# A new issue order for every engine of a fused sparse-attention and MoE kernel, annealed with added latency on transfers

## The chip, the cores and the metric

The kernel runs on one core of a Trainium2 chip. The metric is the device time of one execution in microseconds (us). The engines are TensorE (PE in the profile, its weight loads PEld), VectorE (DVE), ScalarE (ACT), GpSimd (POOL) and SyncE (SP), which here only issues transfers. Each engine works through its own queue strictly in the order in which the program gives it instructions. An instruction whose inputs are not there holds up everything behind it on the same engine.

## The reference, cut to what matters

```python
# q, k, v: (4, 8, 768, 64) f32;  w_in: (512, 2048), w_out: (2048, 512) f32
k_min, k_max = min and max of k over chunks of 32 keys            # 24 chunks
ub   = sum_d max(q*k_min, q*k_max);  ub = where(causal chunk, ub, -1e9)
sel  = the 6 chunks of largest ub for each query
scores = where(sel and causal, q @ k.T / 8, -1e9)
attn = softmax(scores) @ v
x    = attn.transpose(0, 2, 1, 3).reshape(3072, 512)
h    = x @ w_in
out  = (h * clip(h + 3, 0, 6) / 6) @ w_out
```

## The kernel before, in words

The 32 heads are worked in 16 pairs, numbered 0 to 15, four pairs to a batch. The 3072 tokens of the MoE part are worked in 8 groups of 384, two groups to a batch, so a group can start when its batch's four pairs are done. Attention of later batches and MoE of earlier ones are interleaved.

The whole kernel is a list of 1158 tokens, `ORDER`, and a loop that calls one small function for each token, in that order. Nothing reorders afterwards: each function issues its instructions on one engine, so `ORDER`, read for the tokens of one engine, is that engine's queue. Two tokens of different engines may stand in any order as long as a producer stands ahead of its reader.

The tokens, with the engine that runs them (`i` is a pair, `g` a group, a last letter is the PSUM slot: `a`, `b`, `c` are two banks each, `x`, `y` one bank each):

- SP: `lk.i`, `lq.i`, `lv.i` load K, Q, V (two, two and one transfers); `wl.n` loads a quarter of a weight matrix (0 to 3 of w_in, 4 to 7 of w_out); `sm.i` writes a selection mask to DRAM (four transfers) and `ml.i.j` reads it back spread over the rows of key block j; `xt.g` transposes a group's attention output (three transfers); `st.g.t` writes 128 rows of the result (256 KB).
- PE: `K.i`, `Q.i` transpose K and Q; `U.i` (or `ud.i` for two pairs at once) the chunk bounds; `T.i` transposes them, `L.i` the selection; `S.i.u` scores of unit u (six units to a pair); `A.i`, `B.i.e` the products with V for the first and second half of the queries; `X.g.n` transposes for groups 0 and 1; `H.g.f` eight matmuls of the first MoE product; `O.g.t.n` four matmuls of the second one, four such tokens making one output tile of 128 rows. `Z` is a warm-up.
- ACT: `kb`, `qb` copy K and Q out of PSUM as bf16; `rp` is relu(q); `ra` is relu(-q); `ex.i.u` the exponentials of a unit; `hu.g.f` the relu of the gate; `ot.g.t` copies an output tile from PSUM to the buffer that `st.g.t` sends.
- DVE: `mx`, `mn` chunk maxima and minima; `rn` is relu(-q) on this engine, instead of `ra`; `ub`, `us` add the causal bias; `t8` and `sel` select the chunks; `mt` the mask (for pairs 0 to 5 PE adds it to the scores); `mu.i.u` multiplies the exponentials by the mask (pairs 6 to 15); `na`, `nb` normalise; `gt.g.f` the gate's product.
- POOL: `vc.i` casts V, `wc.n` casts a weight quarter, `af.i.u` zeroes what lies above the diagonal in the exponentials, `am.i.j` in the mask.

The buffers that tie the queues together: three PSUM slots of two banks for K, Q, U, S and H; two of one bank for T, L, A, B, X and O; two V staging buffers and two weight staging buffers `WS` (which also hold masks later); and a ring of three output buffers `OT`. `ot` takes the next buffer of that ring, so the fourth `ot` in the list needs the store of the first to have landed:

```python
slot["OT", g, t] = OT[n_ot[0] % 3]
n_ot[0] += 1
```

Of the kernel before, what the change touches and what calls it, by code (L numbers as in the profile page):

```python
# [34 lines left out]
PRD Z.b.14 PRA PRP PRL lk.0 K.0.a kb.0 lq.0 Q.0.b lk.1 rp.0 qb.0 ra.0 K.1.c kb.1 mx.0 mn.0 U.0.a lq.1 Q.1.b rp.1  # L35
qb.1 ra.1 mx.1 ub.0 mn.1 T.0.x lq.2 Q.2.a rp.2 qb.2 U.1.c t8.0 sel.0 lk.2 K.2.b kb.2 lv.1 ub.1 L.0.y mt.0 rn.2
lv.0 S.0.0.c ex.0.0 T.1.x S.0.1.a mx.2 mn.2 ex.0.1 S.0.5.c ex.0.5 lk.4 lq.5 S.0.3.a ex.0.3 lq.4 t8.1 sel.1
S.0.2.b ex.0.2 af.0.1 lk.3 lq.3 U.2.c vc.0 lv.2 ub.2 af.0.5 S.0.4.a ex.0.4 L.1.y mt.1 S.1.5.c ex.1.5 T.2.x wl.1
S.1.1.b t8.2 sel.2 S.1.0.a ex.1.1 ex.1.0 af.0.0 vc.1 af.1.5 S.1.2.c ex.1.2 af.1.1 af.1.0 af.1.2 S.1.3.b ex.1.3
af.1.3 A.0.y L.2.x S.1.4.a ex.1.4 K.4.c mt.2 S.2.1.b Q.4.a kb.4 ex.2.1 na.0 A.1.x Q.3.b B.1.0.y B.1.1.y rp.4  # L40
qb.4 mx.4 mn.4 rp.3 qb.3 ra.3 K.3.c kb.3 rn.4 U.4.a vc.2 lv.3 lv.4 lk.5 lk.6 S.2.5.b ex.2.5 na.1 nb.1 ub.4 mx.3
wl.0 mn.3 af.0.2 S.2.0.a ex.2.0 T.4.x S.2.3.b ex.2.3 t8.4 S.2.4.a ex.2.4 sel.4 S.2.2.c ex.2.2 U.3.b ub.3 Q.5.a
rp.5 qb.5 L.4.y mt.4 lq.8 lk.7 T.3.x t8.3 S.4.0.b lq.6 lq.7 S.4.5.c ex.4.5 af.2.5 af.2.2 sel.3 rn.5 af.0.3
B.0.0.y wc.1 B.0.1.y nb.0 K.5.c L.3.x af.2.1 mt.3 S.4.1.a af.2.0 ex.4.0 kb.5 af.4.0 af.2.3 mx.5 mn.5 ex.4.1
af.4.1 S.4.3.b ex.4.3 X.0.0.y xe.0.0 S.4.2.a ex.4.2 af.4.3 vc.4 A.2.x na.2 wc.0 S.3.0.b ex.3.0 S.3.2.c ex.3.2
U.5.a S.3.3.b A.4.y ub.5 T.5.x na.4 ex.3.3 S.3.1.a ex.3.1 S.4.4.c ex.4.4 S.3.4.b vc.3 S.3.5.a af.3.1 ex.3.5
ex.3.4 t8.5 sel.5 B.2.0.y B.2.1.y L.5.x mt.5 af.4.2 af.4.5 af.3.0 af.3.2 af.3.5 af.3.3 bd K.7.c kb.7 S.5.2.a
nb.2 ex.5.2 A.3.x S.5.0.b ex.5.0 mx.7 mn.7 na.3 B.4.0.y K.6.a kb.6 S.5.5.b ex.5.5 lk.8 wl.2 lv.6 Q.6.c mx.6 mn.6
rp.6 qb.6 B.4.1.y nb.4 rn.6 Q.7.b rp.7 B.3.0.x S.5.1.a ex.5.1 B.3.1.x X.1.0.y qb.7 S.6.0.a ex.6.0 vc.6 wc.2
af.5.2 xe.1.0 wl.3 wc.3 lv.5 wl.4 lq.9 S.5.3.c ex.5.3 rn.7 X.0.1.y xe.0.1 S.7.0.b ex.7.0 nb.3 ud.6.a us.6 wl.5  # L50
lk.9 S.7.2.c ex.7.2 X.1.1.y vc.5 xe.1.1 S.7.1.b S.6.1.a ex.7.1 ex.6.1 af.5.1 af.7.1 af.5.0 af.5.3 af.5.5 wc.4
wc.5 T.6.x T.7.y t8.7 sel.7 t8.6 sel.6 S.6.2.c ex.6.2 S.6.4.b wl.6 ex.6.4 H.0.2.a hu.0.2 gt.0.2 S.5.4.c ex.5.4
H.0.5.b L.6.y L.7.x wc.6 af.7.0 S.6.3.c K.8.a mt.7 hu.0.5 gt.0.5 mt.6 ex.6.3 B.5.0.x kb.8 S.6.5.c mx.8 mn.8
ex.6.5 H.0.7.b hu.0.7 gt.0.7 Q.9.c sm.6 A.5.y na.5 rp.9 qb.9 rn.9 wl.7 H.0.6.a hu.0.6 gt.0.6 ml.6.3 ml.6.0
ml.6.2 H.1.2.b hu.1.2 gt.1.2 Q.8.c rp.8 qb.8 lk.10 rn.8 H.1.0.a hu.1.0 gt.1.0 K.9.b B.5.1.x kb.9 mx.9 mn.9
H.0.0.c hu.0.0 gt.0.0 H.0.1.a hu.0.1 gt.0.1 ud.8.b us.8 H.0.3.c S.8.1.a S.8.0.b ex.8.0 ex.8.1 hu.0.3 wc.7 am.6.3
af.8.0 nb.5 T.8.y O.0.2.0.x H.0.4.b hu.0.4 H.1.4.a t8.8 sel.8 L.8.y gt.0.3 mt.8 gt.0.4 O.0.2.1.x T.9.y t8.9
am.6.2 af.6.1 mu.6.5 sel.9 af.6.0 mu.6.0 hu.1.4 gt.1.4 ml.6.5 ml.6.1 sm.7 ml.6.4 am.6.5 mu.6.2 am.6.4 lq.10
ml.7.5 ml.7.3 ml.7.2 ml.7.4 am.7.4 lk.11 ml.7.0 am.7.2 am.7.5 S.7.4.c ex.7.4 S.8.2.b ex.8.2 mu.6.4 mu.6.1
O.0.2.2.x O.0.2.3.x ot.0.2 S.8.3.c S.8.4.b ex.8.3 ex.8.4 am.7.3 O.0.0.0.y O.0.0.1.y S.7.5.a S.7.3.c ex.7.5  # L60
S.8.5.b ex.8.5 ex.7.3 L.9.x O.0.0.2.y O.0.0.3.y ot.0.0 mu.6.3 mt.9 K.10.a kb.10 mx.10 ml.7.1 mn.10 Q.10.b A.6.x
B.6.0.y H.1.1.c rp.10 qb.10 ra.10 B.6.1.y na.6 hu.1.1 gt.1.1 S.9.1.a ex.9.1 S.9.5.b ex.9.5 O.0.1.0.x S.9.4.a
S.9.0.c S.9.3.b ex.9.3 ex.9.0 ex.9.4 O.0.1.1.x mu.7.5 O.0.1.2.x nb.6 mu.7.4 sm.8 K.11.b mu.7.1 kb.11 mu.7.0
mu.7.2 mu.7.3 O.0.1.3.x ot.0.1 lq.11 Q.11.c rp.11 qb.11 H.1.7.a lv.7 vc.7 af.8.1 mx.11 mn.11 A.7.y na.7 hu.1.7
gt.1.7 ra.11 ml.8.2 ml.8.4 ml.8.3 lq.12 af.9.1 am.8.4 af.9.0 sm.9 xt.2 ml.8.5 am.8.5 lk.12 B.7.0.x B.7.1.x
ml.8.1 ud.10.b nb.7 us.10 S.10.3.c ml.9.3 ml.8.0 ml.9.1 O.1.1.0.y S.10.1.a ml.9.2 ml.9.4 lv.8 st.0.2 ml.9.5
ex.10.3 ex.10.1 S.9.2.b S.10.2.c ex.10.2 ex.9.2 T.10.x t8.10 sel.10 H.1.3.a H.1.5.c hu.1.3 gt.1.3 T.11.x t8.11
sel.11 H.1.6.b hu.1.5 hu.1.6 gt.1.5 gt.1.6 O.1.1.1.y H.2.2.a H.2.7.c L.10.x K.12.b hu.2.2 gt.2.2 mt.10 Q.12.a
af.10.1 hu.2.7 am.8.2 am.8.3 kb.12 rp.12 L.11.x O.1.1.2.y O.1.1.3.y mu.8.5 mt.11 sm.10 gt.2.7 qb.12 mu.8.3 rn.12
mx.12 vc.8 ot.1.1 H.2.1.c mn.12 mu.8.0 mu.8.1 H.2.4.a mu.8.2 O.1.0.0.x O.1.0.1.x O.1.2.0.y H.2.5.b hu.2.4 gt.2.4  # L70
# [12 lines left out]
sel.12 S.13.1.a S.13.2.b ex.13.2 ex.13.1 O.2.1.3.x ot.2.1 B.11.0.y mn.14 B.11.1.y S.14.1.b ex.14.1 S.14.3.c
ex.14.3 nb.11 S.14.2.a ex.14.2 T.13.x lk.15 xt.3 lq.15 xt.5 t8.13 sel.13 L.12.y H.4.1.b hu.4.1 gt.4.1 H.4.0.c
hu.4.0 H.4.7.a hu.4.7 H.4.2.b hu.4.2 gt.4.0 gt.4.7 mt.12 gt.4.2 H.4.4.c hu.4.4 L.13.x H.3.3.a hu.3.3 H.4.3.b
hu.4.3 gt.4.4 gt.3.3 mt.13 lv.12 vc.12 sm.13 lv.13 gt.4.3 H.4.5.c Q.15.a O.4.1.0.y lv.14 sm.12 ml.13.2 st.2.2
st.2.1 ml.12.4 ml.13.0 hu.4.5 gt.4.5 rp.15 qb.15 rn.15 H.4.6.b hu.4.6 ml.12.1 ml.13.4 O.4.1.1.y gt.4.6 K.15.c
H.3.5.a kb.15 mx.15 mn.15 H.3.1.b ml.13.1 O.4.1.2.y O.4.1.3.y ml.13.3 hu.3.5 gt.3.5 hu.3.1 S.13.0.c ex.13.0
gt.3.1 vc.13 ot.4.1 st.4.1 af.13.1 am.12.4 S.14.4.a ud.14.b H.3.2.c am.13.4 vc.14 us.14 T.15.x t8.15 ex.14.4
sel.15 O.4.2.0.y H.3.6.b ml.13.5 ml.12.5 af.12.1 am.12.5 hu.3.6 gt.3.6 L.15.x H.3.0.a hu.3.0 O.4.2.1.y mt.15  # L90
hu.3.2 gt.3.0 T.14.x H.3.7.b H.3.4.a t8.14 sel.14 mu.13.3 ml.12.0 L.14.x O.4.2.2.y O.4.2.3.y hu.3.7 hu.3.4
gt.3.2 mt.14 O.4.0.0.x O.4.0.1.x O.4.0.2.x gt.3.4 O.4.0.3.x gt.3.7 ot.4.2 S.15.3.c S.14.5.a am.13.5 S.14.0.b
af.14.1 am.13.2 mu.12.1 ml.12.2 am.12.2 af.13.0 mu.13.0 ml.12.3 lv.15 am.12.3 mu.12.5 mu.12.4 mu.13.4 mu.12.0
mu.13.2 mu.12.2 mu.12.3 ex.14.0 ot.4.0 ex.14.5 am.13.3 mu.13.5 sm.14 sm.15 st.4.2 ml.14.3 ml.14.2 O.3.2.0.y
# [534 lines left out]
```

## Time and profile before

| | |
|---|---|
| five runs | 284.33, 284.71, 285.49, 287.11, 287.19 us; median 285.49 |
| the profiled execution | 283.86 us, of which the span of instructions is 282.1 |
| granted TensorE clock | 1.000 |
| busy: PE, DVE, ACT, POOL | 270.5, 195.5, 181.9, 73.8 us |
| moved by transfers | 54.38 MB |
| median time from issue to landing: K, Q, V | 4.6, 4.8, 5.8 us |
| the same: a weight quarter, a result store | 7.2 to 7.7, 3.4 us |

The profiled execution is the fastest of the six shown. The 1.8 us between its time and its span lie outside the first and last instruction. Times in the profile count from the start of the span.

### The profile page before, as it was taken

To read this page: it belongs to the slowest core of one execution; us is meant where nothing else is said; L and a number is where in the kernel's file an instruction comes from. 1 tells how busy PE (TensorE), PEld (TensorE's weight loads), DVE (VectorE), ACT (ScalarE), POOL (GpSimd) and SP (SyncE) were. 2 spreads that over 40 slices of the span, in tenths; PEclk is the share of its full clock that TensorE was granted. 3 is DMA by queue.
4 is the path that set the end of the run, shared out by engine and by line. 5 is a ranking of instruction groups with operands and counts; after the bars stand their busy time and mean duration, and the time that the engine had idled before them with its cause. 6 is when DMAs were issued, how large, how long until landed. Compare 5 with 4: busy or idle time off the path is not lost.

```text
span 282.1 us, 6868 instructions
## 1 busy us (share of the span) xinstructions
PE 270.5 (96%) x2670; PEld 162.4 (58%) x2692; DVE 195.5 (69%) x523; ACT 181.9 (64%) x241; POOL 73.8 (26%) x138
## 2 busy tenths in 40 slices
PE   8799999999999999989999999999999999999994
PEld 3567677756654665644655666555455646645541
DVE  4786997988889697879668877659636774625310
ACT  2899999998758897625978876553357522424421
POOL 6043289195451230223142001106315000000000
PEclk9999999999999999999999999999999999999999
DMA  9999998989899998998999496899694120130102
GB/s 167 218 210 212 260 297 185 312 261 326 311 243 254 247 226 127 270 276 235 238 288 257 94 156 136 193 330 258 172 289 172 38 58 0 40 130 37 39 37 112
DMA packets 106911, 54.38 MB, mean 193 GB/s; under 512 B 86912, under 2 KB 95872, under 8 KB 106880
## 3 DMA queue, kind: packets, MB, share of 16 engines
q1 hardware_dynamic: 106880, 53.95, 78.1%
q8 instruction: 21, 0.34, 0.5%
q14 instruction: 10, 0.08, 0.1%
HBM read 42.34 MB, written 9.24 MB: 183 GB/s over the span
## 4 chain that ended last, share of the span: by engine, by line
PE 79%; ACT 8%; DVE 5%; DMA 5%; issue 3%; ACTq 0%
PE PSx L568 13%; PE PSy L568 12%; PE PBa L551 9%; PE PBb L551 9%; PE PBc L551 8%; DMA out_dram<-OT 5%; ACT PT L484 4%; PE PSy L507 3%; PE PSx L507 3%; PE PBa L470 2%; PE PBc L297 2%; PE PBa L297 2%; PE PBc L470 2%; PE PBb L470 2%; PE PBb L289 2%
## 5 line engine op out<-in xcount | busy, mean ns | idle before, releaser
L551 PEld LDWEIGHTS <-WIN 128*128 128x128 bf16 x512 | 48.9, 98 | 34.2 <-issue 1.7
L568 PEld LDWEIGHTS <-GT 128*128 128x128 bf16 x384 | 36.0, 98 | 41.5 <-issue 4.5
L568 PE MATMUL PSy<-WOUT,GT 128*128 128x512 bf16 x181 | 45.6, 379 | 2.2 <-ACT OT L576 1.4
L568 PE MATMUL PSx<-WOUT,GT 128*128 128x512 bf16 x181 | 45.2, 379 | 0.6 <-issue 0.2
L484 ACT ACTIVATE PT<-PBb 128x1024 bf16<-128x1024 f32 (+2 forms) x33 | 30.4, 921 | 7.8 <-PE PBb L470 7.5
L484 ACT ACTIVATE PT<-PBc 128x1024 bf16<-128x1024 f32 (+2 forms) x31 | 30.3, 978 | 7.4 <-PE PBc L470 4.6
L551 PE MATMUL PBa<-XT,WIN 128*128 128x384 bf16 x184 | 33.7, 326 | 0.1
L491 POOL TENSOR_SCALAR_AFFINE_SELECT PT<-PT 128x256 bf16<-128x256 bf16 x56 | 24.0, 449 | 33.4 <-ACT PT L484 29.7
L551 PE MATMUL PBb<-XT,WIN 128*128 128x384 bf16 x168 | 30.7, 326 | 0.0
L562 DVE SCALAR_TENSOR_TENSOR GT<-U,PBa 128x768 bf16<-128x768 bf16 x23 | 21.8, 949 | 12.7 <-ACT U L559 12.6
L551 PE MATMUL PBc<-XT,WIN 128*128 128x384 bf16 x160 | 29.3, 326 | 0.0
L462 DVE TENSOR_TENSOR PT<-PT,WS 128x768 bf16<-128x768 bf16 (+2 forms) x70 | 27.8, 442 | 1.9 <-POOL WS L455 1.9
L559 ACT ACTIVATE U<-PBc 128x768 bf16<-128x768 f32 x20 | 16.3, 813 | 19.8 <-PE PBc L551 19.7
L562 DVE SCALAR_TENSOR_TENSOR GT<-U,PBc 128x768 bf16<-128x768 bf16 x20 | 19.0, 951 | 13.2 <-ACT U L559 13.2
L484 ACT ACTIVATE PT<-PBa 128x1024 bf16<-128x1024 f32 (+2 forms) x32 | 27.7, 867 | 0.4 <-PE PBa L470 0.2
L292 POOL CAST VB<-VS 128x768 bf16<-128x768 f32 x16 | 13.3, 829 | 54.0 <-DMA VS<-in_v_dram 45.3
L559 ACT ACTIVATE U<-PBb 128x768 bf16<-128x768 f32 x21 | 17.0, 812 | 15.8 <-PE PBb L551 14.8
L507 PEld LDWEIGHTS <-PT 128*128 128x128 bf16 x672 | 24.1, 97 | 4.7 <-issue 1.8
L559 ACT ACTIVATE U<-PBa 128x768 bf16<-128x768 f32 x23 | 18.7, 811 | 11.7 <-PE PBa L551 10.2
L562 DVE SCALAR_TENSOR_TENSOR GT<-U,PBb 128x768 bf16<-128x768 bf16 x21 | 20.0, 951 | 6.0 <-ACT U L559 5.7
L470 PEld LDWEIGHTS <-KB 64*128 64x128 bf16 x320 | 14.2, 94 | 14.5 <-issue 10.3
L455 POOL TENSOR_SCALAR_AFFINE_SELECT WS<-WS 128x256 bf16<-128x256 bf16 x30 | 12.7, 437 | 30.3 <-DMA WS<-SCR 29.8
(118 smaller groups left out, 387.9 us busy)
## 6 DMA issues: line engine op xcount, KB each, us to landing
KSM<-in_k_dram SPq DMA_DIRECT2D x32, 192.0 KB, 4.6
QS<-in_q_dram SPq DMA_DIRECT2D x32, 192.0 KB, 4.8
VS<-in_v_dram SPq DMA_DIRECT2D x16, 384.0 KB, 5.8
out_dram<-OT SPq DMA_DIRECT2D x24, 256.0 KB, 3.4
WS<-in_moe_w_in_dram SPq DMA_DIRECT2D x4, 1024.0 KB, 7.2
WS<-in_moe_w_out_dram SPq DMA_DIRECT2D x4, 1024.0 KB, 7.7
SCR<-MTM SPq DMA_DIRECT2D x40, 72.0 KB, 3.6
MX<-SCR SPq DMA_DIRECT2D x10, 288.0 KB, 5.3
```

What stands on the lines that cost most here:

```text
L292: nc.gpsimd.tensor_copy(VB[i % 4][:, :, :, 0:D], VS[i % 2][:].rearrange("p e j d -> p j e d"))
L297: nc.tensor.transpose(flat[:, j * P:(j + 1) * P], src[:, j].rearrange("p e d -> p (e d)"), IDENT32[:])
L455: nc.gpsimd.affine_select(out=T, in_=T, pattern=[[0, 2], [1, P]], compare_op=A.is_ge, fill=0.0, base=0, channel_multiplier=-1)
L462: nc.vector.tensor_tensor(out=T, in0=T, in1=mask_view(i, j, lo, q0 + n), op=A.mult)
L470: nc.tensor.matmul(PSB[c][:, e, at:at + n], lhsT=K[rows, j * P:(j + 1) * P], rhs=Q[rows, q0:q0 + n], start=True, stop=q0 + n <= Q0 or i in ...
L484: nc.scalar.activation(PT[i % 3][u][:, :, 0:n], PSB[slot["S", i, u]][:, :, 0:n], ACT.Exp, scale=float(scale))
L491: nc.gpsimd.affine_select(out=T[:, :, lo:lo + P], in_=T[:, :, lo:lo + P], pattern=[[0, 2], [1, P]], compare_op=A.is_ge, fill=0.0, base=0, ...
L507: nc.tensor.matmul(O[:, e, t, :], lhsT=PT[i % 3][u][:, e, lo:lo + P], rhs=VB[i % 4][:, j, e, :], start=(j == 0), stop=(j == qb))
L551: nc.tensor.matmul(PSB[c][:, ff, 0:GRP], lhsT=WIN[:, kt, (2 * f + ff) * P:(2 * f + ff + 1) * P], rhs=XT[g % 3][:, kt, :], start=(kt == 0), ...
L559: nc.scalar.activation(slot["R", g, f][:], PSB[slot["H", g, f]][:, :, 0:GRP], ACT.Relu, bias=3.0)
L562: nc.vector.scalar_tensor_tensor(out=GT[g % 2][:, 2 * f:2 * f + 2, :], in0=slot["R", g, f][:], scalar=6.0, in1=PSB[slot["H", g, f]][:, :, ...
L568: nc.tensor.matmul(PSS[c][:], lhsT=GT[g % 2][:, f, t * P:(t + 1) * P], rhs=WOUT[:, f, :], start=(f == 0), stop=(f == FT - 1))
```

## The change

`ORDER` is replaced; no function changes. The new list was found by annealing in a model that adds latency to every transfer. It has the same 1158 tokens but for relu(-q): before, `ra` (ACT) does it for pairs 0, 1, 3, 10, 11, 13, 14 and `rn` (DVE) for the other nine; after, `ra` for 1, 2, 10, 11, 12, 14, 15. PSUM slots change with the order. Every engine's queue is permuted: in the built program all 2692 matmuls are there as before, and SP issues the same 230 transfers in another sequence.

The parts of the list that the steps below speak of (the start; the first weight quarter; the stores of groups 0 to 2; the last transposes):

```diff
-PRD Z.b.14 PRA PRP PRL lk.0 K.0.a kb.0 lq.0 Q.0.b lk.1 rp.0 qb.0 ra.0 K.1.c kb.1 mx.0 mn.0 U.0.a lq.1 Q.1.b rp.1
-qb.1 ra.1 mx.1 ub.0 mn.1 T.0.x lq.2 Q.2.a rp.2 qb.2 U.1.c t8.0 sel.0 lk.2 K.2.b kb.2 lv.1 ub.1 L.0.y mt.0 rn.2
-lv.0 S.0.0.c ex.0.0 T.1.x S.0.1.a mx.2 mn.2 ex.0.1 S.0.5.c ex.0.5 lk.4 lq.5 S.0.3.a ex.0.3 lq.4 t8.1 sel.1
...
-H.0.5.b L.6.y L.7.x wc.6 af.7.0 S.6.3.c K.8.a mt.7 hu.0.5 gt.0.5 mt.6 ex.6.3 B.5.0.x kb.8 S.6.5.c mx.8 mn.8
...
-ml.8.1 ud.10.b nb.7 us.10 S.10.3.c ml.9.3 ml.8.0 ml.9.1 O.1.1.0.y S.10.1.a ml.9.2 ml.9.4 lv.8 st.0.2 ml.9.5
...
-af.10.1 hu.2.7 am.8.2 am.8.3 kb.12 rp.12 L.11.x O.1.1.2.y O.1.1.3.y mu.8.5 mt.11 sm.10 gt.2.7 qb.12 mu.8.3 rn.12
-mx.12 vc.8 ot.1.1 H.2.1.c mn.12 mu.8.0 mu.8.1 H.2.4.a mu.8.2 O.1.0.0.x O.1.0.1.x O.1.2.0.y H.2.5.b hu.2.4 gt.2.4
-mu.8.4 hu.2.1 gt.2.1 hu.2.5 gt.2.5 mu.9.1 am.9.3 ml.9.0 am.9.4 am.9.2 st.0.0 lv.9 O.1.2.1.y H.2.0.a mu.9.3
...
-S.11.4.c ex.11.4 af.12.0 am.10.4 mu.10.3 mu.10.4 mu.10.1 mu.10.2 ml.11.1 st.1.1 S.11.0.a S.11.5.b ex.11.5
-O.2.0.3.y ot.2.0 K.13.c kb.13 Q.13.b rp.13 qb.13 A.10.x O.2.2.0.y vc.11 O.2.2.1.y ex.11.0 ml.11.3 ml.11.5
...
-H.6.3.b B.15.1.x nb.15 H.6.1.c hu.6.1 O.5.2.2.y H.6.4.a hu.6.4 B.14.0.x gt.6.1 B.14.1.x nb.14 gt.6.4 xt.7
-O.5.2.3.y H.6.2.c H.6.7.a hu.6.3 ot.5.2 gt.6.3 hu.6.2 st.5.1 H.6.6.b O.6.0.0.x O.6.2.0.y hu.6.6 hu.6.7 gt.6.2
-O.6.0.1.x O.6.0.2.x O.6.2.1.y gt.6.7 gt.6.6 O.6.0.3.x H.7.4.c hu.7.4 gt.7.4 H.7.7.a H.7.5.b hu.7.5 gt.7.5 hu.7.7
...
+PRD Z.b.14 PRP PRL PRA lk.0 K.0.a lq.0 kb.0 mx.0 mn.0 Q.0.b rp.0 qb.0 lk.1 K.1.c rn.0 U.0.a ub.0 kb.1 mx.1 lq.1
+Q.1.b T.0.x mn.1 t8.0 sel.0 lq.2 Q.2.a lk.2 lv.0 lq.3 lk.3 lv.1 rp.1 qb.1 ra.1 U.1.c ub.1 lk.4 vc.0 lv.2 lq.4
+rp.2 qb.2 ra.2 K.2.b kb.2 L.0.y mt.0 S.0.1.c ex.0.1 S.0.2.a T.1.x S.0.3.c ex.0.2 ex.0.3 S.0.5.a ex.0.5 mx.2 mn.2
...
+t8.3 af.1.3 sel.3 af.2.2 af.1.5 K.4.c lq.5 kb.4 mx.4 S.2.3.b Q.4.a ex.2.3 B.0.0.y L.3.x mt.3 rp.4 lk.5 wl.0 lv.4
+lq.7 S.2.1.b ex.2.1 vc.1 wc.0 af.2.0 af.1.2 af.2.1 B.0.1.y qb.4 mn.4 A.1.x S.3.1.b ex.3.1 S.3.2.c ex.3.2 S.2.5.b
...
+Q.5.b B.1.0.x L.4.y rp.5 mt.4 qb.5 B.1.1.x mn.5 S.4.2.c af.3.0 ex.4.2 rn.5 A.2.y lv.3 S.3.3.a ex.3.3 af.2.5 lk.7
...
+ot.0.1 st.0.1 sm.8 st.0.0 lk.12 nb.6 S.9.3.a S.9.5.c S.9.2.b ex.9.3 mu.7.4 mu.7.3 mu.7.1 mu.7.0 ex.9.5 ex.9.2
...
+lv.8 ex.9.1 mu.7.2 mu.7.5 ex.9.0 sm.9 A.7.x B.7.0.y us.10 na.7 xt.2 B.7.1.y st.0.2 nb.7 S.10.1.c ex.10.1
...
+O.1.1.0.x ot.1.2 kb.12 L.11.y H.2.7.c mx.12 ml.9.4 lq.12 mn.12 hu.2.7 gt.2.7 H.2.6.a hu.2.6 mt.11 H.2.4.b
...
+am.9.2 mu.9.0 mu.8.4 mu.8.5 O.1.0.1.y O.1.0.2.y Q.12.b O.1.0.3.y ml.9.1 sm.10 ot.1.0 lv.9 st.1.2 rp.12 H.2.5.a
...
+mu.9.1 S.11.5.a S.11.0.b ex.11.0 S.10.3.c ex.10.3 O.1.1.3.x O.2.2.0.y O.2.2.1.y ot.1.1 ex.11.5 ml.10.3 sm.11
+S.10.2.b ex.10.2 S.11.4.c S.11.1.a ex.11.1 ex.11.4 O.2.2.2.y O.2.2.3.y ot.2.2 ml.10.1 A.9.x na.9 af.11.0 vc.10
...
+H.6.2.c H.6.5.a B.15.1.y O.5.0.1.x O.5.0.2.x O.5.0.3.x hu.6.3 hu.6.5 nb.15 hu.6.2 gt.6.2 gt.6.3 O.6.1.0.y ot.5.0
+O.6.0.0.x H.6.4.c hu.6.4 gt.6.5 gt.6.4 O.6.0.1.x O.6.1.1.y H.6.6.b hu.6.6 gt.6.6 xt.7 st.5.2 H.7.4.a hu.7.4
```

## The prediction, made before the run

> **What bounds the kernel now.** I read the page first, then PE's waits, then ACT's, then the timelines where those waits lie, and last the queue of transfers.
>
> From the page: busy time, the slices of ACT, the granted clock, the share of the transfer engines.
>
> ```profile
> PE 270.5 (96%) x2670; PEld 162.4 (58%) x2692; DVE 195.5 (69%) x523; ACT 181.9 (64%) x241; POOL 73.8 (26%) x138
> ACT  2899999998758897625978876553357522424421
> PEclk9999999999999999999999999999999999999999
> DMA  9999998989899998998999496899694120130102
> ```
>
> PE is the bound overall, at full clock. ACT is full too in slices 2 to 8 (about 14 to 63 us). Transfers keep their engines full for 150 us. The table of stages says it for ACT (columns: PE, PEld, DVE, ACT, POOL busy; clock; transfer share; GB/s):
>
> ```profile
> 20.00:40.00 20.00, 18.89 (x322) 14.31 (x322) 15.64 (x61) 19.77 (x27) 8.84 (x18) 1.00 1.04 246
> 40.00:60.00 20.00, 19.78 (x370) 14.65 (x369) 16.36 (x45) 19.73 (x27) 12.49 (x23) 1.00 1.02 265
> ```
>
> Busy PE is not PE at its peak. So I took each PE token's slot, from its first matmul to the next token's (an H token 1.300 us, an O token 0.863), and the median slot of each kind. The 384 tokens sum to 269.0 us of such slots; they took from 1.29 to 278.5. The excess, 7.9 us by the table, lies at 0 to 40 us (4.4: start and ACT), 60 to 80 (1.0), 120 to 160 (2.5), and nearly nowhere else. The Trainium skill ("Perfetto Trace Analysis", Identifying the Most-Contended Engine) would judge PE by LDWEIGHTS busy, here 58%, and so leave 42% of the span, 118 us, as headroom. The slots leave 8; I go by them, since a new order cannot shorten a slot.
>
> PE's waits, ACT's waits, then both timelines at the two places:
>
> ```profile
> PE PSy L568 <- ACT OT L576: 1.4, 2, 1.0
> ACT OT L576 <- DMA out_dram<-OT: 6.2, 2, 5.1
> ...
> 124.28 0.60 ACT L576 ACTIVATE OT<-PSy 128x512 f32<-128x512 f32 x1 [5.12 <-DMA out_dram<-OT]
> 124.93 1.02 PE L568 MATMUL PSy<-WOUT,GT 128*128 128x512 bf16 x4 [1.01 <-ACT OT L576]
> ...
> 146.83 0.60 ACT L576 ACTIVATE OT<-PSy 128x512 f32<-128x512 f32 x1 [1.10 <-DMA out_dram<-OT]
> 147.48 2.75 PE L568 MATMUL PSy<-WOUT,GT 128*128 128x512 bf16 x11 [0.43 <-ACT OT L576]
> ```
>
> The first pair is ot.1.1. It needs the OT buffer of st.0.2, which was issued late:
>
> ```profile
> 116.73 7.46 DMA out_dram<-OT
> ...
> 141.18 5.57 DMA out_dram<-OT
> ```
>
> The two rows (start, us from issue to landing) are from the chain that ended last. ACT stands 5.12 us, and O.1.2.0 waits 1.01 us for its PSUM slot. The second pair above is ot.2.0 behind st.1.1, the second row here: 0.43 us on PE. These are PE's only waits over 0.15 us after 60 us with another engine as releaser.
>
> **The change, part by part.** No instruction is added or removed but six relu(-q) that swap engines, three each way. So the sum is: waits that go, waits that come, and where ACT leads.
>
> *1. The two store waits: −1.6.* I gave each transfer its queue time, the spacing of landings in the trace where the queue is full (lk 1.75, lq 1.72, lv 1.8, a mask load 0.6 to 1.3, a store 0.72; wl 4.2 and xt 3.9 taken between two such spacings), and summed it over everything issued up to it. From that I subtracted the PE slots (fast ones, the 20th percentile) ahead of its reader. The result, the transfer's debt, must stay below what PE itself has fallen behind its slots (12 at 80 us, 13.5 at 120, 15 to 17 at 140 to 155). Before: st.0.2 has 17.4 against 13.5 (it waits), the stores ahead of ot.2.0 and ot.2.2 have 15.1 and 15.5 against about 15.5 (the edge; one waits). After: st.0.0 and st.0.1 are issued around sm.8, straight after their copies, st.0.2 behind xt.2, and no store of groups 0 and 1 has a debt over 2.7; the largest of any store is 8.9 (st.2.0). Both waits go: 1.01 + 0.43, and with them two short ones just behind (0.09 before H.2.3, 0.11 before S.12.2). What is late next at O.1.2 is nothing near: ACT has 5 us of idle time there and DVE is 15 us ahead by the same count.
>
> A rule that speaks against this step: the Trainium skill ("DMA: Bandwidth & Descriptors", Anatomy of one DMA — SWDGE (gpsimd) path) fits a transfer as 2.0 us plus bytes over 436 GB/s, 2.6 us for a store of 256 KB. With it st.0.2 lands at 119.3, before ACT could want the buffer; no wait, and the step is worth 0. The row has 7.46. The rule is for another queue kind and a lone transfer: the last store here, alone, does land about 2 us after issue. The row decides.
>
> *2. The other loads: 0.* Largest debts before and after: Q and K loads 13.8 to 10.4, V 13.7 to 10.0, masks 12.5 to 8.6, the transposes 13.1 to 10.0, weights 9.7 to 10.1. No PE wait in the trace is charged to them except 0.3 at K.1, so 3 to 4 us more of margin is worth nothing in this execution. In an execution with later landings it is worth what those would cost.
>
> *3. The start: +0.35.* ra.0 leaves ACT and rn.0 joins DVE behind mn.0 (9.8 to 10.55), so the second half of U.0 starts at 10.6 instead of 10.35, Q.1 a quarter later, rp.1 at 12.0 instead of 11.74. ra.2 joins ACT (0.54) ahead of kb.2. The first exponential starts at about 16.3; before it was 15.97. From there ACT is the bound, with idle times of 0.2 us at most until 66, so the delay stays. Nothing hides it.
>
> *4. The ACT stage: −0.1.* ACT's summed slots up to ex.6.3, where PE last waits for ACT's stage, are 53.4 us; PE slots from the first token that waits for it (S.6.5) to the end are 205.4: 258.8. After, ex.6.3 comes after 50.6 us of ACT, and 208.1 of PE are left from H.1.3: 258.7. More MoE work is left behind ACT's stage, and less ACT work is ahead. The relus that swap are inside these sums. DVE takes one more in this stage (0.67); it has 4 us to spare (its summed slots less PE's are −4.6 at worst, at T.3, against ACT's −0.9 at H.1.3), and without that cover it would cost its 0.67.
>
> *5. POOL behind the first weight quarter: 0, from 0 to +5.* In POOL's queue wc.0 stands ahead of af.2.0, af.1.2 and af.2.1, and PE's B.1.0 needs af.1.2. So B.1.0, and with it everything on PE, now waits for wl.0 to land. Before, wc.1 stood likewise ahead of af.2.1 and af.2.0, but their reader A.2 came 2 us of PE slots later. wl.0 is the 28th transfer, with 4.6 MB up to it, which had landed at about 34 us before. Then wc.0 takes 1.89, af.2.0 and af.1.2 1.1: ready at 37. PE reaches B.1.0 after 30.3 us of slots, with 8 of lag, at 38.3. Cover 1.3 us, and ACT has about 2 us queued beyond that.
>
> *6. The end: 0.* xt.7 waits for nb.15; H.7.4 needs it. The PE slots between B.15.1 and H.7.4 shrink from about 10 (counted from B.14.1, the later one before) to 8.6 us. nb.15 (0.78), and 5.0 from the first issue to the last landing of xt.7 in the trace, need about 6. If the cover went, each us beyond 8.6 would be one on the end. Behind it the tail is the same: four O tokens, a copy, a store.
>
> **Sum.** 283.86 − 1.6 + 0.35 − 0.1 = 282.5 us. The profiled execution is 1.63 under the median of the runs shown. I take the forecast for the median of the new runs: I expect them near their own profile, because the spread before (284.3 to 287.2) is what a queue at the edge of its debts would give.
>
> **The rivals.**
> *More goes.* The excess at 0 to 40 and 60 to 80 us is half order, not work: 2.2 + 0.5 less gives 279.8. For it: PE's waits on a K load, on DVE (1.0 at U.0) and on ACT (0.55 at Q.4) lie there. Against: ACT is full from 16 us on, and its sum is unchanged by 4.
> *Nothing comes of it.* The store waits go, but the spread of the runs is not due to transfers; 285.49 − 1.6 + 0.25 = 284.1, and if ACT stands once more for a late mask or a slot, 285. For it: PE's own waits on transfers are so small.
> *Slower.* Point 5 with a late wl.0. It decides from a landing at 36 (B.1.0 waits), costs the end from about 38 on (ACT's backlog spent), us for us; at 41 the gain is eaten. Landing at 44, as with the before kernel's wl.0 (42.3) and a little more, gives 282.5 + 6 = 288.5. For it: a weight quarter takes 7.2 us from issue. Against: only 27 transfers are ahead of it, 33 before.
> *The order does not take hold.* The queues follow the list token by token, so I give this nothing.
>
> **Chances.** Forecast 0.50 (its own range 280.9 to 284.2), more goes 0.25, nothing 0.16, slower 0.09. About 1% is what a measurement of this kernel tells from no change, 282.6 below. Faster by over 1%: all of "more" and 0.33 of the forecast, 0.58. Within: 0.17 + 0.16 = 0.33. Slower: 0.09. The range cuts a tenth at each end: 279.3 to 286.0.
>
> **What would show it.** Right: no wait of OT for out_dram on ACT and none of PSy or PSx for OT on PE; the slots' excess at 120 to 160 us down from 2.5 to under 1; ACT's first exponential at 16.3 and ACT at 19.7 of 20 in both stages above; no wait of PE for POOL at B.1.0. Wrong: a PE wait charged to PT L491 near 38 us, a wait of XT before H.7.4 near 250, ACT idle over 1 us between 20 and 60, or a first H token later than before's (62 us).

## The result, and the profile after

| | us, median (range) | executions | against before |
|---|---|---|---|
| before | 285.21 (282.91 to 289.9) | 77 | 1 |
| after | 283.21 (281.62 to 284.74) | 42 | 0.993, 95% interval 0.9916 to 0.9944 |

The change makes the kernel 2.0 us faster, 0.7%. The forecast was 282.5, in a range of 279.3 to 286.0. The runs also stand closer together: 26 of the 77 executions of before took over 286 us, none of after took over 284.74. The ratios here and below are of the executions that lie within 1.5% of the fastest of their kernel, so they are not the quotients of the medians.

The profiled execution of after took 284.05 us, with a span of 281.7. Its page, the lines that answer to those of before:

```profile
PE 270.7 (96%) x2672; PEld 163.4 (58%) x2692; DVE 194.8 (69%) x523; ACT 182.0 (65%) x241; POOL 72.2 (26%) x138
ACT  2599999998758988453888855844658434333321
DMA  8999999995899979699999799998699320211022
```

The work is the same, so the sums are. The granted clock is full in every slice, and the transfers still fill their engines for 150 us. What moved is seen by stage (columns: PE, PEld, DVE, ACT, POOL busy; clock; transfer share; GB/s):

```profile
20.00:40.00 20.00, 18.69 (x324) 13.74 (x313) 15.50 (x62) 19.57 (x26) 11.20 (x23) 1.00 1.07 237
40.00:60.00 20.00, 19.36 (x381) 15.10 (x385) 16.18 (x42) 18.99 (x26) 12.94 (x26) 1.00 1.01 274
120.00:160.00 40.00, 39.45 (x396) 22.99 (x399) 30.54 (x71) 28.32 (x38) 10.89 (x23) 1.00 0.99 238
```

The same late stage of before:

```profile
120.00:160.00 40.00, 38.04 (x382) 21.79 (x385) 31.61 (x77) 28.05 (x38) 10.36 (x20) 1.00 0.99 235
```

PE is 1.4 us busier there in after. In the two early stages ACT is less busy than before (19.77 and 19.73): it lost 0.2 and 0.7 us. PE's waits in after, and the one wait of ACT for a store (releaser; us in total, times, longest):

```profile
PE PBa L366 <- ACT KB L318: 1.5, 1, 1.5
PE PBb L289 <- DVE MX L262: 1.3, 1, 1.3
PE PBc L366 <- DVE KM L343: 0.6, 1, 0.6
...
ACT OT L576 <- DMA out_dram<-OT: 3.2, 1, 3.2
```

No wait of PE for a copy of OT is left. The three PE waits listed lie in the first 15 us, and no other is over 0.53. One store still holds ACT for 3.2 us, and nobody on PE waits for that copy.

To compare both executions I used **PE's lag**: the start of a token less the sum of the fast slots (20th percentile of the kind) ahead of it. At 10, 80, 120, 160 us and the end it was 2.98, 12.05, 13.49, 17.41 and 18.61 in before; 3.87, 13.57, 15.47, 17.22 and 18.20 in after. So after has lost 1.5 us more by 80, gains 2.2 between 120 and 160, and ends 0.4 ahead. Of the 1.5, 0.87 are the chip's and not the order's: the warm-up matmuls took 5.95 us from first start to next token, against 5.08, because PE came to full speed later in that execution (last section). So the order has lost 0.65 by 80 us. With the same start the two spans would differ by 1.3 us.

### The profile page after: what moved, and what is told of

Same layout as the page of the kernel before. It is cut to its first block, busy times and chain, and to the rows that moved or that the text cites. A ratio compares the mean times of both kernels' runs of the same rounds, so it can differ in the third digit from the quotient of the medians.

```text
span 281.7 us, 6892 instructions
## 1 busy us (share of the span) xinstructions
PE 270.7 (96%) x2672; PEld 163.4 (58%) x2692; DVE 194.8 (69%) x523; ACT 182.0 (65%) x241; POOL 72.2 (26%) x138
## 4 chain that ended last, share of the span: by engine, by line
PE 76%; ACT 7%; DVE 6%; DMA 5%; issue 2%; SPq 1%; POOL 1%; POOLq 0%; ACTq 0%; DVEq 0%
PE PSy L568 13%; PE PSx L568 11%; PE PBb L551 11%; PE PBa L551 9%; PE PBc L551 9%; ACT PT L484 4%; PE PSx L507 3%; DMA KSM<-in_k_dram 3%; PE PBa L297 3%; PE PBb L289 2%; PE PBc L470 2%; DMA VS<-in_v_dram 2%; PE PSy L507 2%; DVE KM L343 2%; PE PBa L470 2%
## 5 line engine op out<-in xcount | busy, mean ns | idle before, releaser
L568 PEld LDWEIGHTS <-GT 128*128 128x128 bf16 x384 | 36.0, 98 | 39.8 <-issue 2.5
L568 PE MATMUL PSy<-WOUT,GT 128*128 128x512 bf16 x198 | 49.3, 379 | 0.5 <-issue 0.2
L568 PE MATMUL PSx<-WOUT,GT 128*128 128x512 bf16 x166 | 40.9, 379 | 0.6 <-issue 0.2
L551 PE MATMUL PBb<-XT,WIN 128*128 128x384 bf16 x192 | 35.1, 326 | 0.0
L559 ACT ACTIVATE U<-PBb 128x768 bf16<-128x768 f32 x24 | 19.5, 812 | 16.6 <-PE PBb L551 16.6
L551 PE MATMUL PBa<-XT,WIN 128*128 128x384 bf16 x160 | 29.3, 326 | 0.0
L562 DVE SCALAR_TENSOR_TENSOR GT<-U,PBb 128x768 bf16<-128x768 bf16 x24 | 22.8, 950 | 8.9 <-ACT U L559 8.7
L462 DVE TENSOR_TENSOR PT<-PT,WS 128x256 bf16<-128x256 bf16 (+2 forms) x70 | 27.8, 445 | 0.3 <-POOL WS L455 0.3
L491 POOL TENSOR_SCALAR_AFFINE_SELECT PT<-PT 128x256 bf16<-128x256 bf16 x56 | 22.0, 415 | 17.9 <-ACT PT L484 17.7
L562 DVE SCALAR_TENSOR_TENSOR GT<-U,PBa 128x768 bf16<-128x768 bf16 x20 | 19.0, 950 | 10.6 <-ACT U L559 10.5
L292 POOL CAST VB<-VS 128x768 bf16<-128x768 f32 x16 | 13.7, 857 | 45.9 <-DMA VS<-in_v_dram 45.9
L559 ACT ACTIVATE U<-PBa 128x768 bf16<-128x768 f32 x20 | 16.3, 813 | 13.7 <-PE PBa L551 13.3
```

The source lines that it names most:

```text
L292: nc.gpsimd.tensor_copy(VB[i % 4][:, :, :, 0:D], VS[i % 2][:].rearrange("p e j d -> p j e d"))
L462: nc.vector.tensor_tensor(out=T, in0=T, in1=mask_view(i, j, lo, q0 + n), op=A.mult)
L491: nc.gpsimd.affine_select(out=T[:, :, lo:lo + P], in_=T[:, :, lo:lo + P], pattern=[[0, 2], [1, P]], compare_op=A.is_ge, fill=0.0, base=0, ...
L551: nc.tensor.matmul(PSB[c][:, ff, 0:GRP], lhsT=WIN[:, kt, (2 * f + ff) * P:(2 * f + ff + 1) * P], rhs=XT[g % 3][:, kt, :], start=(kt == 0), ...
L559: nc.scalar.activation(slot["R", g, f][:], PSB[slot["H", g, f]][:, :, 0:GRP], ACT.Relu, bias=3.0)
L562: nc.vector.scalar_tensor_tensor(out=GT[g % 2][:, 2 * f:2 * f + 2, :], in0=slot["R", g, f][:], scalar=6.0, in1=PSB[slot["H", g, f]][:, :, ...
```

## The experiments

The ratios are against before on the same chip; the medians of different chips are not to be compared. Before's own median was 286.14 us beside the first four kernels of the table, 285.77 beside the next four, 285.09 beside the last four. Where a difference from after is given in us below, it is the difference of the two ratios, of 285.2. Lines of the first four kernels stand 4 lower than in the listing (a shorter order list), those of the two with a larger store 1 higher.

| kernel | median us | ratio to before (95%) |
|---|---|---|
| e1_stores_early | 286.21 | 1.0003 (0.997 to 1.0036) |
| e2_beforehead_aftertail | 288.06 | 1.0071 (1.0046 to 1.0097) |
| e3_afterhead_beforetail | 292.81 | 1.0219 (1.0159 to 1.0279) |
| e5_start_relus | 283.88 | 0.9886 (0.9835 to 0.9938) |
| before_ot4 | 285.01 | 0.9965 (0.9932 to 0.9998) |
| before_1mb | 289.54 | 1.0124 (1.0088 to 1.0161) |
| after_1mb | 286.20 | 1.0010 (0.9988 to 1.0032) |
| after_store_late | 287.53 | 1.0025 (0.9994 to 1.0056) |
| before_half_loads | 282.03 | 0.9897 (0.9855 to 0.9938) |
| after_half_loads | 282.61 | 0.9925 (0.9899 to 0.9951) |
| after_wl0_late | 293.88 | 1.0318 (1.0274 to 1.0361) |
| after_ot4_ra0 | 283.26 | 0.9937 (0.9914 to 0.9961) |

### The stores moved up, alone

```
 SP's list of before (only the stores move)
- ... lv.8 st.0.2 ml.9.5 ... lv.9 (st.0.0) ... ml.10.3 st.0.1 ... ml.11.1 st.1.1 ... st.1.0 st.1.2
+ st.0.2 behind ot.0.2; st.0.0 behind sm.8; st.0.1 behind sm.9;
+ st.1.1 behind ot.1.1; st.1.0 and st.1.2 behind lk.13
```

> The order of before, with only six stores moved forward in SP's list: st.0.2 right after its copy, st.0.0 behind sm.8, st.0.1 behind sm.9, st.1.1 right after its copy, st.1.0 and st.1.2 behind lk.13. Theory (the late gain is the store waits, and the runs of before above 286 us are the same stores at the edge): 1.5 us under before, about 283.7, no wait of OT for out_dram on ACT between 110 and 160 us, the lag of PE at 160 us about 1.5 below before's 17.4, and no run above 286. Rival A (the gain comes from the compute order or from the margins of the other loads): within 0.4 us of before, the lag comes back somewhere else by 160. Rival B (the runs above 286 have nothing to do with the stores): some of them stay, whatever the median does.

Measured: no gain; the interval leaves room for 0.9 us at most, and 1.5 was expected. My theory of the stores alone fell here. The profiled execution is one of the longer ones (288.15), so its waits may be larger than the usual ones. ACT's wait for out_dram is gone from the trace, but PE's waits show what came instead:

```profile
PE PSy L503 <- POOL VB L288: 2.3, 1, 2.3
...
PE PBb L293 <- DMA QS<-in_q_dram: 1.1, 1, 1.1
```

The first is A.7, which stands 2.3 us for the cast of V of pair 7. Two stores now go ahead of its load lv.7. How little room there was, before itself tells, in the timelines of POOL and PE (start, us):

```profile
102.71 0.83 POOL L292 CAST VB<-VS 128x768 bf16<-128x768 f32 x1 [6.65 <-DMA VS<-in_v_dram]
...
103.61 0.53 PE L507 MATMUL PSy<-VB,PT 128*128 128x65 bf16 x12
```

POOL begins the cast when lv.7 lands, ends at 103.54, and PE takes A.7 at 103.61. It shows as no wait, and it has 0.07 us of margin. In e1 the cast starts at 106.26. In after, lv.7 lands at the same 102.7 and A.7 comes at 108.42, 4.8 us after the cast. **In this full queue, moving stores up made the loads behind them late.**

### The two hybrids

```
e2: [before up to ot.0.2] + [rest as in after], st.0.2 behind ot.0.1
e3: [after up to nb.5]    + [rest as in before]
```

> The list of before up to ot.0.2 (about 88 us), then the rest in the order of after; st.0.2 put right after ot.0.1, since the ring of OT starts with another copy here. Theory (the two parts add: the late part is worth 2.2, the early part of the change gives back about 0.9 by the start's relus and by ACT's idle times at 37 to 51 us): the best of all, 0.9 under after, about 282.3. Rival (the early part of after prepares the late gain by its margins of loads): no better than after, 283.2 or above, with transfers as releasers on PE or ACT behind 90 us.

> The other hybrid: the list of after up to nb.5 and its tail (about 80 us), then the rest in the order of before, late stores included. Theory: the worst, before plus 0.9, about 286.1, with the wait of ot.1.1 for st.0.2 back and runs above 287. Rival (the early part makes the margin that the stores lacked): under before, 284 or less, no such wait.

Both are slower than either parent, so they don't tell whether the parts add. In e3 most of it is the seam: behind it DVE and ACT have other work in front than PE expects, and PE waits 1.9 and 1.8 us for GT. In e2 PE waits 2.1 us for GT at S.7.3; its profile had lost more than that ahead of the seam already. What e3 does show is the late part of before again: its two waits of PSy for OT, 2.2 us in all, are back behind the head of after, which rules out that the early part makes the room for the stores.

e2 gave something not looked for. Up to 88 us its list is before's, token by token, and yet PE stands at K.5, where before did not:

```profile
39.78 0.85 PE L293 MATMUL PBc<-IDENT,KSM 128*128 128x128 f32 x6 [1.87 <-DMA KSM<-in_k_dram]
```

lk.5 landed at 39.6 here, at 37.7 in the profile of before. **The same transfer behind the same list lands up to 3.5 us apart** from one execution to the next: in the five profiles here that share before's list up to 88 us (before, e1, e2 and two below), lv.3 was issued between 26.2 and 26.7 us and landed between 33.1 and 36.6. Lateness is then handed on: lk.9 landed at 71.1 in before, 71.9 in e1 and 73.9 in e2, each time 8.1 to 8.2 us after its issue. This made the next theory, L: before has several loads with no margin, and what it loses in a typical execution is more than its one profiled execution shows.

### The store waits taken away without moving a transfer

```
-    OT = ring(3, [P, DMODEL], FP32, "OT")
+    OT = ring(4, [P, DMODEL], FP32, "OT")
```

(and `n_ot[0] % 4` where the buffer is chosen)

> Before, with four buffers of OT in place of three, the order untouched: ot.1.1 gets a buffer that was never used, ot.2.0 the one of st.0.1. No transfer moves. Theory S (the stores alone, as in the prediction): both waits of OT for out_dram are gone and the time is 1.4 to 1.6 us under before, most of the way to after. Theory L (formed after the first four kernels: landings come up to 3 us later in some executions, and before has loads at their edge there, so that the margin of all loads is what after gains): the waits are gone but at most 0.7 us comes of it, and the spread of the runs stays.

Measured: 1.0 us under before, with an interval from 0.1 to 1.9. Both waits for OT are gone. The lag at 160 us is 16.64 against 17.41: 0.8 gained of the 1.44, because S.12.3, at 135 us, now stands for DVE:

```profile
PE PBa L470 <- DVE GT L562: 0.9, 1, 0.9
```

So by this number the stores are worth about half of what the change brings. The interval is wide enough for either theory; what speaks for L is the spread, which stays: the single executions still reach 287.01.

### The same extra transfer in both kernels

```
+    def dummy_store():
+        nc.sync.dma_start(DUM[:], WIN[:, 0:2, :])
 ORDER: ... sm.8
+ dd
```

> Before, with one store more in SP's list, of 1 MB from two quarters of WIN to a scratch tile in DRAM that nobody reads, right behind sm.8 (about 95 us): some 4.2 us of queue time at the rate of that stretch, all transfers behind it that much later. Theory L (before has no margin left behind 95 us): 3 to 5 us over before, with PE waiting for V, Q or masks or for OT. Rival (margins do not matter, the queue catches up before anybody waits): within 1 us of before.

> After, with the same store of 1 MB at the same place, right behind sm.8 (about 105 us here). Theory L (after has 4 us more of margin ahead of its loads): at most 1 us over after, 0.993 to 0.997 of before. Rival (its margin lies elsewhere, or the same few transfers set the time): as much slower as the other one, 3 to 5 us, over 1.004 of before.

Before loses 3.5 us (2.5 to 4.6), as theory L has it, and at once: the loads of Q.11 and of V for A.7 are the next in the queue.

```profile
PE PBc L298 <- DMA QS<-in_q_dram: 2.1, 1, 2.1
PE PSy L508 <- POOL VB L293: 1.6, 1, 1.6
PE PSy L569 <- ACT OT L577: 1.6, 2, 0.8
```

After loses 2.3 us (1.0010 − 0.993, of 285.2; about 1.5 to 3.0), more than the 1 us expected. That is less than before loses, but the intervals overlap, so the times of this pair don't decide between the two theories. In its trace only one late transfer matters, xt.2, which H.2.7 waits for. In the profile of after xt.2 had landed at 117.0 and H.2.7 started at 118.9, so it had 1.9 us of room and not 4; here it lands at 122.1. And here the wait costs more than its length (two stretches of 3.41 us, columns as above):

```profile
PE PBc L552 <- DMA XT<-XB: 1.9, 1, 1.9
...
119.18:122.59 3.41, 1.48 (x10) 0.73 (x9) 1.82 (x2) 1.29 (x2) 0.00 (x0) 1.00 0.60 141
122.59:126.00 3.41, 3.41 (x13) 1.66 (x11) 0.42 (x1) 0.81 (x1) 0.00 (x0) 0.50 0.84 224
```

The granted clock is the third figure from the right: 1.00, then 0.50 from 122.59 to 126.00, which is 1.7 us lost on top of the 1.9. This is the longest of the 22 executions (288.47) and the only one of them with a mean clock as low as 0.994, which is what one such stretch makes of 286 us. So the fall of the clock is no part of the median's 2.3.

### One store late in after

```
- ... st.0.1 sm.8 st.0.0 lk.12 ...
+ ... st.0.1 sm.8 lk.12 ... st.0.2 ml.9.2 st.0.0 ml.8.3 ...
```

> After, with one store moved: st.0.0 from behind sm.8 to behind ml.9.2, nine entries of SP's list later, so that it lands at about 121 us; ot.1.2 wants its buffer at 117.9 and PE's next user of that PSUM slot, L.11, follows 0.9 us later. Theory S: ACT waits 3 us and PE 2 to 2.5 of them, 2 us over after, about 1.000 of before. Rival (a late store only idles ACT, and the transfers that move up repay PE): within 0.5 us of after, 0.993.

(The store moves back by six entries of SP's list, not nine.)

Measured: 2.7 us over after. PE waits for the copy that waits for the store, and the clock falls behind it:

```profile
PE PSy L426 <- ACT OT L576: 3.5, 1, 3.5
...
121.00:122.00 1.00, 0.83 (x5) 0.49 (x5) 0.15 (x1) 0.81 (x2) 0.00 (x0) 0.50 0.88 302
```

Of 22 executions, 15 show a mean clock of 0.994 or less, with a median of 287.74; the other 7 have 284.81. So a late store does reach PE. Executions without the fall of the clock are 1.6 us over after's median of 283.21, those with it 4.5; in the profile the wait is 3.5 us and the half clock behind it costs 1.6.

### The queue relieved in both kernels

```
-        for e in range(2):
+        for e in range(2 if i < 3 else 1):
             nc.sync.dma_start(dst[:, :, e, :], x[b, 2 * hp + e]...
```

> Before, with only one of the two heads of Q and K loaded for the pairs 3 to 15 (the other half of each staging tile keeps older data, so the values are not the reference's; no engine does less). 26 transfers of 256 KB go, some 23 us of queue time. Theory L (what after gains is room ahead of its transfers): with a queue that is never full before stops losing anything to it, 282.3 to 283.2, ratio 0.988 to 0.992, level with the next kernel within 0.5 us. Rival C (after's compute order is 2 us better by itself): stays 1.5 to 2 us above the next kernel.

> After, with the same halved loads of Q and K for the pairs 3 to 15 (values not the reference's for the same reason). Theory L: after has little to gain, 0.3 to 0.8 us, 282.4 to 282.9, ratio 0.989 to 0.992, no better than the kernel above. Rival C: 1.5 to 2 us under the kernel above.

(A transfer of Q or K here is 192 KB, not the 256 of the expectation; 5.1 MB of 54.4 go. Both kernels leave out half of Q and K from pair 3 on, so they serve for the times alone.)

**This settles it.** With room in the queue, before takes 282.03 us (281.41 to 282.57) and after 282.61 (281.96 to 283.34). Before gains 3.1 us by median, and all six of its executions lie under the fastest of before beside them (283.50); after gains hardly anything (0.9925 against 0.993). Rival C, a better compute order, wanted after 1.5 to 2 us ahead: it is behind by median, and the intervals leave it 0.6 ahead at most. That less traffic makes every engine faster is ruled out by after, which had the same relief. PE's waits in the relieved before name neither a transfer nor OT:

```profile
PE PBb L289 <- DVE MX L262: 1.3, 1, 1.3
PE PBa L366 <- DVE KM L343: 1.2, 1, 1.2
PE PBa L297 <- ACT PT L484: 0.6, 1, 0.6
```

The lags of the two (80 us: 12.11 and 12.83; end: 17.14 and 17.09) show the price of after's order too. Less the warm-up (5.50 and 5.25 us) they are 6.61 and 7.58 at 80 us, 11.64 and 11.84 at the end: 1.0 us lost in the early part, most of it given back in the late one.

**The early part shows theory L in the traces alone.** Take PE's lag at 80 us less the warm-up, against that of before's own profile. With before's list it is the same in e1, and 0.5, 1.2 and 2.8 us more in before_ot4, before_1mb and e2. With after's list it is 0.6 to 0.7 more each time (after, after_1mb, after_store_late, after_half_loads). After pays a little every time; before pays nothing or much. One of the readers is K.5 in e2, above. Another is B.5.0 in before_1mb, well ahead of the extra store, behind the load of V for pair 6 (landed at 58.9, in before at 57.0):

```profile
59.06 0.83 POOL L293 CAST VB<-VS 128x768 bf16<-128x768 f32 x1 [7.50 <-DMA VS<-in_v_dram]
...
66.91 0.54 PE L508 MATMUL PSx<-VB,PT 128*128 128x65 bf16 x12 [1.41 <-POOL PT L492]
```

POOL has no pause between the two, so PE's 1.4 us are the load's.

### The first weight quarter late

```
- ... lk.5 wl.0 lv.4 lq.7 lv.3 lk.7 lk.6 lq.8 lq.6 ...
+ ... lk.5 lv.4 lq.7 lk.7 lk.6 lq.6 wl.0 lv.3 lq.8 ...
```

> After, with the load wl.0 moved in SP's list behind lv.4, lq.7, lk.7, lk.6 and lq.6 (lv.3 follows it): it lands near 42.5 us in place of 33.4. Point 5 of the prediction: wc.0 ends at 44.5, af.1.2 at 45.6, B.1.0 is reached at about 39.8; ACT's backlog covers 2 us of that, the rest goes to the end us for us: 4 us over after, ratio 1.007. Rival (PE's and ACT's queued work covers it): within 0.5 us of after, 0.993 to 0.995.

Measured: 11.1 us over after, not 4. wl.0 landed at 44.9. POOL and PE:

```profile
44.95 1.89 POOL L255 CAST WIN<-WS 128x2048 bf16<-128x2048 f32 x1 [13.59 <-DMA WS<-in_moe_w_in_dram]
...
47.98 0.23 PE L507 MATMUL PSx<-VB,PT 128*128 128x65 bf16 x1 [8.12 <-POOL PT L491]
```

The chain is that of point 5, and its price was too low on two counts. Nothing covers B.1.0: PE takes tokens in order, so ACT runs dry once the scores already made are used up, and all 8.1 us go to the end. Then the clock:

```profile
44.00:48.00 4.00, 0.03 (x1) 0.03 (x2) 0.00 (x0) 0.00 (x0) 3.05 (x5) 0.50 0.70 131
48.00:52.00 4.00, 4.00 (x55) 3.05 (x55) 2.71 (x7) 1.02 (x1) 3.62 (x8) 0.50 0.86 292
52.00:56.00 4.00, 4.00 (x68) 2.22 (x66) 1.69 (x8) 2.95 (x4) 0.28 (x1) 0.75 1.07 330
```

PE works at half speed from 48 to 54: 3 us. 8.1 + 3 make the 11.1.

### The start, and a try at both

```
e5:            - rn.0 (DVE), ra.2 (ACT)   + ra.0 behind qb.0, rn.2 behind mt.0
after_ot4_ra0: - rn.0 (DVE)               + ra.0 behind qb.0, and ring(4, ...) for OT
```

> After, with the relus of the pairs 0 and 2 as in before: ra.0 on ACT behind qb.0 in place of rn.0 on DVE, rn.2 on DVE behind mt.0 in place of ra.2 on ACT. Theory (step 3 of the prediction): 0.35 us under after, about 282.85, the first exponential 0.35 to 0.4 earlier after the same release of the clock. Rival (the stage of ACT swallows it): within 0.15 us of after; ACT idles longer between 35 and 52 us instead.

> After, with ra.0 on ACT behind qb.0 in place of rn.0 on DVE (ra.2 stays on ACT), and four buffers of OT. In the profiles so far the second half of U.0 follows the start of Q.0 by 3.32 us with ra.0 and by 3.57 with rn.0, so 0.25 should be saved; the wait of OT for out_dram that is left in after (3.2 us of ACT) has no reader on PE, so its going is worth 0. Expected: 0.25 under after, ratio 0.991 to 0.993. Rival (the store margin still costs in the executions with late landings): 0.7 us or more under after, 0.990 or less, with a narrower spread.

Neither can be told from after: the intervals overlap widely. In e5's trace the second half of U.0 follows the start of Q.0's transposes by 3.32 us (11.09 − 7.77), in after by 3.57 (11.49 − 7.92), so ra.0 saves its 0.25. But rn.2 on DVE then holds S.0.2 for 0.4. The kernel with ra.0 alone and four buffers comes to 0.9937, after to 0.993, with the same spread: the room for stores in after is enough as far as this shows, and no version here is shown to beat it.

## Why the prediction came out as it did

**The total.** Profile against profile and with the same warm-up time, the span fell by 1.3 us; the sum had 1.35. That they agree so well is luck. By the lags the early part took 0.65 (the sum had 0.25), the stretch from 80 to 120 us took 0.5 (no term), 120 to 160 gave 2.2 (the sum had 1.6), and the rest gave 0.2. The forecast for the median has luck in it too. It stood 3.0 under the median on the page, 1.63 of them because it took the profiled execution of before, one of its good ones, as the level of all executions of after. What late landings cost before thus came in through the base, while step 2, where it belongs, had 0. Between medians the fall is 2.0, and 0.7%: the 0.58 given to "faster by over 1%" was too much.

**Step 1, the store waits (−1.6).** The mechanism is right: both waits of PE are gone, and with the waits alone removed (before_ot4) 1.0 of the 1.6 comes, with an interval that holds 1.6. "Nothing near" held for O.1.2; the next to be late came 11 us on, S.12.3 for GT, with 0.9 us. The ruler of debts found the right stores. Of the signs, the excess at 120 to 160 us did fall below 1 (0.8 over the median slots, from 2.9 by the same count). One sign failed in part: a wait of OT for out_dram, 3.2 us, is left on ACT, without a reader on PE. The row was rightly put above the rule: stores in this queue take a median of 3.4 us and up to 7.5, and after_store_late shows that PE pays for one.

**Step 2, the other loads (0). This is the term that was wrong.** The debts were right (V 13.7 against a lag of 13; A.7 in before had 0.07 us of margin), and so was the sentence that later landings would cost. But the term was set to 0, since one profile showed no wait. Landings differ by up to 3.5 us between executions, so loads at the edge cost in many of them: 0 to 2.8 us by 80 us in the five profiles of the same list. What before loses to transfers is 3.1 us by the relieved pair; less the 1.0 of the stores, some 2 belong to the other loads. That split rests on a difference with an interval of nearly 1 us on either side; that the whole is transfers does not.

**Step 3, the start (+0.35).** From the start of Q.0's transposes to the first exponential: 15.97 − 7.03 = 8.94 in before, 17.23 − 7.92 = 9.31 in after. +0.37.

**Step 4, the ACT stage (−0.1).** Mis-sized: the early part took 0.65 in the profiled pair and 1.0 in the relieved one, so 0.3 to 0.6 for this step beside the start. The sum took ACT as continuously busy; in after it has gaps of about 0.3 us at 37, 42, 45 and 51 us, at 37 and 45 for scores and at 51 for a transpose of K that PE makes too late. The sign I had set for it, ACT at 19.7 of 20 in both stages, failed with 19.57 and 18.99. Two signs of being wrong came true as well: ACT idle for 1.4 us in all between 20 and 60 (0.5 in before), and a later first H token, at 62.9 against 60.0 (the 62 given there for before was wrong).

**Step 5, POOL behind wl.0 (0).** Right in after: wl.0 landed at 33.4 (34 estimated), the cast ended at 35.3, and B.1.0 started at 39.8 without a wait. The price of the rival was off by more than a factor of two, as the late wl.0 shows.

**Step 6, the end (0).** Right: xt.7 landed at 247.6, H.7.4 started at 250.2.

**The rivals.** "More goes" did not happen; the early lag grew. "Nothing comes of it" rested on a spread that is not due to transfers. It is: relieve the queue, and 281.4 to 282.6 is left of 283.5 to 290.6. Its time, 284.1, was nearer to the result than the 279.8 of "more goes" all the same, because it started from the median.

## What to carry to other kernels

A load that lands just in time shows no wait in the profile, and is paid for in the executions that the profile did not catch. Compare each landing with its reader, and count what is closer than the spread of landings between executions of the same list (here up to 3.5 us) as a cost already. Where the list stays the same, several profiles of it show that cost better than one. In a full queue, look for room by issuing less work ahead of the tight readers or by having the readers come later; moving stores up did not give it here. And the quick test of whether room is what an order lacks is to make the transfers smaller, or one of them larger, in both orders.

## What the runs showed of the hardware

**A wait of PE can cost nearly twice its length, and it matters where it lies.** Behind the waits of 1.9, 3.5 and 8.1 us above, the granted clock was 0.5 for 3.4 us or more, so that 1.6 to 3 us were lost at full work. Waits of 2.3 us (A.7 in e1), 2.1 (Q.11 in before_1mb, S.7.3 in e2) and 1.9 (K.5 in e2) kept the clock at 1.00.

The traces tell what sets them apart. Their clock changes only at the edges of windows of 3.41 us, counted from its release at the start: 34 windows from 6.54 to 122.59 us in after_1mb, 34 from 4.89 to 120.94 in after_store_late, 26 from 4.09 to 92.83 in e3, 11 from 6.21 to 43.76 in after_wl0_late. So I took PE's idle time inside each window. In after_1mb the whole wait lies in one (119.18 to 122.59, 1.93 idle). The longer wait in e1 is cut by an edge at 105.90, into 1.10 and 1.24:

```profile
102.48:105.90 3.42, 2.31 (x16) 1.49 (x15) 1.94 (x3) 3.32 (x6) 0.00 (x0) 1.00 0.89 239
105.90:109.31 3.41, 2.17 (x74) 1.80 (x73) 1.58 (x4) 0.34 (x1) 2.31 (x5) 1.00 0.90 179
```

In the fourteen traces, start and end of the program aside, the clock fell behind each window with 1.82 us of idle PE or more (1.82 in e3, 1.93 in after_1mb, 3.24 in after_store_late, 3.41 in after_wl0_late) and behind none with 1.71 or less. At the end of the program, in after_half_loads, a window with 1.99 kept it, so the limit is not exact, and four falls are few. The Trainium skill ("TensorE: Matmul & The Clock Gate", Part 1: The HAM clock gate) has a window of about 3.4 us that runs freely and halves the clock after an idle one. The length of the window agrees; that it has to be idle as a whole does not: about half was enough.

Of the 117 executions of before beside the experiments, 14 had a mean clock of 0.994 or less, each 287.36 us or longer; of the 64 of after and after_ot4_ra0, none. That a fall of the clock behind a late transfer makes these long executions is likely, but no trace of one is there. It is not the whole of the spread: 46 of the 117 took over 286 us, and 32 of these had a higher clock.

**PE comes to full speed at no fixed time.** The 14 warm-up matmuls took between 4.56 and 6.14 us in the timelines of fourteen profiles, and what follows shifts with it unless a load is waited for instead. Before and then after:

```profile
1.29 5.24 PE L289 MATMUL PBb<-MX 128*128 128x512 bf16 x14 [1.29 <-DVE MX L262]
```

```profile
1.29 6.14 PE L289 MATMUL PBb<-MX 128*128 128x512 bf16 x14 [1.29 <-DVE MX L262]
```

One matmul starts every 0.43 us up to 5.5 us in before, and every 0.22 from there on. In after all of them keep to 0.43; its clock is released at 7.3, when the last has started. The profile's windows give the clock as 1.00 before the release too, so at the start the spacing tells and the clock column doesn't. The same section of the page lets the point depend on where the free-running window stands when PE starts. Here 0.87 us of it lay between the two profiles to be compared, two thirds of the difference that was to be found.
